# Reading the moving operand of seven products with a step of eight elements, in an attention and mixture-of-experts kernel

## The chip, the cores and the metric

The kernel runs on one core of one Trainium2 chip. The metric is the time of one execution on the device in microseconds. Each kernel is run several times and the median is given. Beside these runs there is one profiled execution, whose trace records every instruction of every engine; its own time is given with it.

The engines of the core work side by side, each through its own queue of instructions: TensorE (PE in the profile; PEld is its loading of the stationary operand), VectorE (DVE), ScalarE (ACT), GpSimd (POOL) and SyncE (SP, which here only issues DMAs). TensorE reads its operands from SBUF and writes PSUM; the stationary operand is loaded first, and the moving operand is then streamed past it, one column after the other.

## The reference

Attention in chunks of 64 tokens gives x of 4608 x 512. Each token then goes to the one of eight experts that its cosine router picks, and is scaled by its gate.

```python
def _attn_ref(q, k, v):                      # (8, 8, 576, 64) each
    q_c = q.reshape(B, H, nc, chunk, D)      # chunk = 64, and k_c, v_c alike
    scores = scale * np.matmul(q_c, k_c.transpose(0, 1, 2, 4, 3))
    attn = np.exp(scores - np.max(scores, axis=-1, keepdims=True))
    attn = attn / (np.sum(attn, axis=-1, keepdims=True) + 1e-09)
    return np.matmul(attn, v_c).reshape(B, H, S, D)

def _moe_ref(x, expert_emb, tau, w1, w2):    # N, D, E, F = 4608, 512, 8, 1024
    logits = xn @ en.T / tau                 # rows of x and expert_emb at norm 1
    expert_idx = np.argmax(logits, axis=1)
    probs = softmax(logits)
    gate_w = probs[np.arange(N), expert_idx]
    for e in range(E):
        mask = expert_idx == e
        h = np.maximum(x[mask] @ w1[e], 0.0)
        out[mask] = gate_w[mask, None] * (h @ w2[e])
```

All operands are float32. The change lies in `x[mask] @ w1[e]` and the maximum with 0 behind it.

## The kernel before

**Two stages.** The first, some 200 us, is attention for 36 tiles of 128 tokens, with the router: each token's row, with its logits and its number, is scattered to a list in device memory (`spots`) that is sorted by expert. The second takes the lists back in blocks of 128 rows: two groups of 64 tokens, `s` = 0 and 1, each of one expert, so that a block can have two experts at once. There are 36 paired blocks and a tail whose number is only known when the kernel runs. The order of the instructions is written out by hand (a manual schedule), so each engine's queue is the order of the calls.

**The first layer of a block** is `hidden_fast` (line 328) for 33 of the blocks. It computes two-by-two blocks with seven products in place of eight: the rows' halves and the weights' halves are first combined (`add_x`, line 307, on the tokens; `add_up`, line 283, on the weights), seven products p1 to p7 are formed, and their sums are the four quarters of the hidden layer. The other blocks use `hidden_part` (line 237), the plain product, which the change leaves as it is.

**A product** (line 335) takes one PSUM bank `ps` of 128 partitions x 256 columns, in rotation out of six. It consists of 8 calls of matmul (line 342): two steps `c` over the contraction, two groups `s`, and two halves `r` of the weights' columns. A call has 128 rows of contraction, 32 columns of the stationary operand (32 tokens of `a`) and 256 columns of the moving operand (256 hidden units of `w`). Its output lies on 32 partitions of the bank, and calls that write different quarters of the partitions run side by side. In the trace each float32 call is two matmuls.

**The order of the columns.** The 256 hidden units of one call are counted `(i k)`: `i` of 32, `k` of 8, with `k` the faster. The second layer needs the hidden layer transposed, 32 x 32 at a time, with the 32 columns of one square being those of one `k`. So the columns have to be brought into the order `(k i)` on the way. Before, the products are computed in the order `(i k)`, and `relu` (line 359) turns it: it reads its input with a step of eight elements and writes it without one.

**Behind the products.** p1 is copied from PSUM to SBUF by ACT (line 377). VectorE adds the others to it (`add`, line 374, each 128 x 256), so that `C` in SBUF holds four quarters. ACT applies the relu to each quarter in two halves of 64 partitions (line 361), eight instructions a block, reading `C` and writing `h`. VectorE transposes `h` to `hT` in two instructions (`turn`, line 368), which read `h` without a step.

**The second layer** is `result` (line 405): 32 calls of 512 columns on line 413, 64 matmuls in the trace, then a scaling by the gate on ACT (line 421), and a scatter of the rows to the output (line 428, on POOL's queue). The loop at line 1121 issues, for each block j, first the products of block j + 1 and then the result of block j, so that TensorE has the result to work on while ACT and VectorE turn the products of the next block.

**Other work in the queues.** In ACT's queue between the relus stand the gate's square root and exponential, each with a load of its table (lines 224 and 231), and, if an expert changes, three copies of its new weights (`take_next`, line 295; copies on line 301 under a condition on a register, line 299). On VectorE the next block's tokens are transposed (line 203, with a step of four elements in its input).

Of the kernel before, what the change touches and what calls it, by code (L numbers as in the profile page):

```python
# [12 lines left out]
AF = mybir.ActivationFunctionType  # L13
# [12 lines left out]
def kernel(  # L26
# [21 lines left out]
    G = P // 2  # L48
    Q = 32
# [226 lines left out]
    def block(s, m, w1=None):  # L276

        if m in TS:
            return sums_sb[s][:, TS.index(m)]
        u, v = UV[m]  # L280
        return (w1 or w1_sb)[s].rearrange("p (u c) (v x) -> p u v c x", u=2, v=2)[:, u, v]
# [22 lines left out]
    def quarters(xT):  # L304
        return xT.rearrange("p (u c) (s b i) -> p u b c s i", u=2, s=2, b=2)
# [17 lines left out]
    def bank(ps_h, shape):  # L323
        tag = f"h{bank_no[0] % 6}"
        bank_no[0] += 1
        return ps_h.tile(shape, FP32, tag=tag, name=tag)

    def hidden_fast(j, ps_h, gate, turn_next, swap_next):

        d = mo[j]  # L330
        x = quarters(d["xT"])
        s1, s2, s3, s4 = d["S"]
        W2 = KF * Q

        def product(a, m):
            ps = bank(ps_h, [P, W2])
            for c in range(KD // 2):
                for s in range(2):
                    w = block(s, m)[:, c].rearrange("p (r x) -> p r x", r=2)
                    for r in range(2):  # L340
                        t0 = G * s + Q * r
                        nc.tensor.matmul(  # L342
                            ps[t0 : t0 + Q],
                            lhsT=a[:, c, s],
                            rhs=w[:, r],
                            start=c == 0,
                            stop=c == KD // 2 - 1,
                        )
            return ps


        last = "_last" if j == LEAST - 1 else ""
        hT = bp.tile([P, KF, P], FP32, tag="hT" + last, name="hT", bufs=1 if last else 2)
        d["hT"] = hT
        C = late_p.tile([P, 4, W2], FP32, tag="C", name="C")
        U, c11, c12, c22 = (C[:, i] for i in range(4))
        h = [late_p.tile([P, 2, W2], FP32, tag=f"h{b}", name=f"h{b}") for b in range(2)]

        def relu(b, v, x):
            for s in range(2):  # L360
                nc.scalar.activation(  # L361
                    h[b][G * v : G * v + G, s].rearrange("p (k i) -> p k i", i=Q),
                    x[G * s : G * s + G].rearrange("p (i k) -> p k i", i=Q),
                    AF.Relu,
                )

        def turn(b):
            nc.vector.transpose(  # L368
                hT.rearrange("p k (s b i) -> p b s k i", b=2, i=Q)[:, b],
                h[b].rearrange("p s (k i) -> p s k i", i=Q),  # L370
            )

        def add(out, a, b, op=ALU.add):
            nc.vector.tensor_tensor(out, a, b, op)  # L374

        p1 = product(x[:, 0, 0], "B11")
        nc.scalar.copy(U, p1)  # L377
        next(gate, None)
        next(gate, None)
        p2 = product(x[:, 1, 0], "B21")  # L380
        add(c11, U, p2)
        next(gate, None)
        relu(0, 0, c11)
        turn_next()
        p3 = product(s4, "B22")
        p5 = product(s1, "T1")
        p6 = product(s2, "T2")
        add(U, U, p6)
        add(c12, U, p5)
        add(c12, c12, p3)  # L390
        relu(0, 1, c12)
        for _ in gate:
            pass
        p7 = product(s3, "T3")
        add(U, U, p7)
        add(c22, U, p5)
        relu(1, 1, c22)
        p4 = product(x[:, 1, 1], "T4")
        swap_next()
        add(U, U, p4, ALU.subtract)  # L400
        relu(1, 0, U)
        turn(0)
        turn(1)
# [42 lines left out]
    with (  # L446
# [577 lines left out]
        for t in range(-3, NT + 3):  # L1024
# [22 lines left out]
            if 0 <= t < NT:  # L1047
                values(t)
                b = (2 * t + 2) // NCB + 1
# [52 lines left out]
    with (  # L1102
# [18 lines left out]
        for j in range(LEAST - 1):  # L1121
            n = j + 2

            def turn_next():
                if n < LEAST:
                    turn_xb(n)
                    if n + XBUF < NJ:
                        load_x(n + XBUF)
                    add_x(n)

            def swap_next():
                if NE <= n < LEAST:
                    take_next(n)
# [93 lines left out]
```

## Time and profile before

| | |
|---|---|
| runs before the change | median 677.75 us of 14 (674.63 to 680.26) |
| profiled execution, whole time | 674.17 us |
| its span, first to last instruction | 672.4 us |
| mean granted TensorE clock | 0.981 |
| line 342, matmuls of the products | 3696, mean 379 ns |
| line 413, matmuls of the result, 512 columns | 2304, mean 594 ns |
| line 361, relu on ACT, 64 x 256 | 264, mean 678 ns, 179.0 us busy |

Matmuls overlap each other, so the busy time of one group of them says little; the time from the start of one stretch to the start of the next does more. The busy share of an engine is taken over the whole span; in the second stage it is read from a window. An instruction's idle time is that of its engine just before it, with the instruction whose end released it.

### The profile page before, as it was taken

What the parts mean: (1) busy time and instruction counts of PE and PEld (TensorE: products, weight loads), DVE (VectorE), ACT (ScalarE), POOL (GpSimd) and SP (SyncE); (2) the same over time, 40 slices, a digit from 0 to 9 for tenths busy, and PEclk for the clock granted to TensorE, in tenths of its full rate; (3) what the DMA queues carried; (4) which work ended last, traced back from release to release, by engine and by line L of the source; (5) the groups of instructions that cost most, each with busy time, mean ns of one, the idle gap of its engine ahead of it and who ended that gap; (6) DMA issues with size and microseconds to landing.
All of it is one profiled execution on the core that took longest, in us unless ns stands there. A gap on an engine that the chain in (4) does not pass through costs nothing. (4 is left out here: it accounts for less than half of the span.)

```text
span 672.4 us, 24844 instructions
## 1 busy us (share of the span) xinstructions
PE 625.5 (93%) x9744; PEld 350.0 (52%) x9744; DVE 421.4 (63%) x1140; ACT 444.5 (66%) x776; POOL 155.4 (23%) x237
## 2 busy tenths in 40 slices
PE   6869999998898979999999999999999999999993
PEld 5658878785443446666434444334444444444441
DVE  4648888986498536557675566767654666564430
ACT  5536767765225847777877867778777777877740
POOL 7828787843310100000100100000001000100101
PEclk9879999998999989999999999999999999999997
DMA  9977999988918711112786111776821114411101
GB/s 253 252 197 218 284 283 292 280 237 339 355 53 295 295 34 46 47 36 92 292 308 224 50 39 45 282 280 216 328 81 56 37 48 164 169 43 34 50 30 36
DMA packets 94590, 112.66 MB, mean 168 GB/s; under 512 B 52364, under 2 KB 72588, under 8 KB 94456
## 3 DMA queue, kind: packets, MB, share of 16 engines
q1 hardware_dynamic: 82728, 72.84, 34.1%
q0 software_dynamic: 11696, 38.04, 16.9%
q8 instruction: 81, 1.33, 0.8%
q14 instruction: 53, 0.43, 0.2%
q10 hardware_dynamic: 32, 0.02, 0.0%
HBM read 334.71 MB, written 22.69 MB: 532 GB/s over the span
## 5 line engine op out<-in xcount | busy, mean ns | idle before, releaser
L413 PE MATMUL y_ps<-w,hT 128*32 128x512 f32 (+1 forms) x2368 | 273.1, 589 | 3.7 <-DMA w<-in_moe_w_dram 3.7
L361 ACT ACTIVATE h<-C 64x256 f32<-64x256 f32 x264 | 179.0, 678 | 95.2 <-DVE C L374 68.7
L413 PEld LDWEIGHTS y_ps<-w,hT 128*32 128x32 f32 x2368 | 93.5, 110 | 153.9 <-issue 123.8
L428 POOL DMA_INDIRECT out_dram<-y,spot x36 | 34.9, 968 | 437.6 <-ACT C L377 186.8
L374 DVE TENSOR_TENSOR C<-C,h 128x256 f32<-128x256 f32 x231 | 96.1, 416 | 49.4 <-DVEq L299 42.6
L342 PE MATMUL h<-w,S 128*32 128x256 f32 x1056 | 98.1, 379 | 1.8 <-DVE w L291 1.8
L342 PE MATMUL h<-sums,xbT 128*32 128x256 f32 x1056 | 97.0, 379 | 0.0
L342 PE MATMUL h<-w,xbT 128*32 128x256 f32 x1056 | 79.4, 380 | 7.1 <-ACTq L299 5.9
L368 DVE STREAM_TRANSPOSE hT<-h 128x512 f32<-128x512 f32 x66 | 46.7, 708 | 44.2 <-ACT h L361 44.1
L342 PEld LDWEIGHTS h<-w,xbT 128*32 128x32 f32 x1056 | 40.9, 110 | 43.2 <-ACTq L299 13.4
L342 PEld LDWEIGHTS h<-w,S 128*32 128x32 f32 x1056 | 49.3, 110 | 24.3 <-DVE w L291 1.5
L342 PEld LDWEIGHTS h<-sums,xbT 128*32 128x32 f32 x1056 | 49.0, 110 | 21.8 <-ACT C L377 0.4
L227 DVE TENSOR_SCALAR rn<-rn 128x1 f32<-128x1 f32 x37 | 5.7, 153 | 72.5 <-ACT rn L224 72.5
L342 PE MATMUL h<-sums,S 128*32 128x256 f32 x528 | 48.7, 379 | 0.0
L682 ACT COPY xT<-tr 128x512 f32<-128x512 f32 x36 | 21.1, 587 | 35.9 <-PE tr L680 35.9
L800 POOL DMA_INDIRECT spots<-xr,dest x36 | 37.1, 1029 | 33.1 <-DVE dest L765 9.9
L203 DVE STREAM_TRANSPOSE xbT<-xin 128x256 f32<-128x256 f32 x73 | 44.3, 645 | 0.5 <-DVE hT L368 0.5
L224 ACT ACT_TABLE_LOAD x34 | 43.6, 1283 | 0.9 <-issue 0.3
L421 ACT ACTIVATE y<-y_ps,gate 128x512 f32<-128x512 f32 (+1 forms) x37 | 25.2, 682 | 28.6 <-issue 15.2
L231 ACT ACT_TABLE_LOAD x34 | 43.6, 1283 | 0.6
L572 POOL DMA_DIRECT2D kx<-in_k_dram x36 | 31.5, 876 | 17.0 <-PE tr L595 16.9
L572 POOL DMA_DIRECT2D qx<-in_q_dram x40 | 34.4, 863 | 0.9 <-PE tr L595 0.6
(202 smaller groups left out, 800.6 us busy)
## 6 DMA issues: line engine op xcount, KB each, us to landing
w<-in_moe_w_dram SPq DMA_DIRECT2D x74, 2048.0 KB
next_w<-in_moe_w_dram SPq DMA_DIRECT2D x67, 2048.0 KB
xin<-spots SPq DMA_DIRECT2D x158, 64.0 KB
qx<-in_q_dram POOLq DMA_DIRECT2D x32, 256.0 KB
v<-in_v_dram SPq DMA_DIRECT2D x56, 144.0 KB
kx<-in_k_dram POOLq DMA_DIRECT2D x28, 256.0 KB
spot<-spots SPq DMA_DIRECT2D x80, 4.0 KB
spots<-blank SPq DMA_DIRECT2D x2, 576.0 KB
```

The costliest lines, as they stand in the source:

```text
L203: nc.vector.transpose(xT[:, :, cols].rearrange("p c (b i) -> p b c i", i=Q), t[:, s * (D // 2) : (s + 1) * (D // 2)].rearrange("p (b i c) ...
L224: nc.scalar.activation(rn, spot[:, j % SPOTS, SQ : SQ + 1], AF.Sqrt)
L231: nc.scalar.activation(sh, sh, AF.Exp, accum_out=gate)
L342: nc.tensor.matmul(ps[t0 : t0 + Q], lhsT=a[:, c, s], rhs=w[:, r], start=c == 0, stop=c == KD // 2 - 1,)
L361: nc.scalar.activation(h[b][G * v : G * v + G, s].rearrange("p (k i) -> p k i", i=Q), x[G * s : G * s + G].rearrange("p (i k) -> p k i", i=Q),
L368: nc.vector.transpose(hT.rearrange("p k (s b i) -> p b s k i", b=2, i=Q)[:, b], h[b].rearrange("p s (k i) -> p s k i", i=Q),)
L374: nc.vector.tensor_tensor(out, a, b, op)
L413: nc.tensor.matmul(ps[Q * r : Q * r + Q, 0:w], lhsT=d["hT"][:, c, Q * t0 : Q * t0 + Q], rhs=w2_sb[s][buf_of(j)][:, c, d0 : d0 + w], start= ...
L421: nc.scalar.activation(y[:, 0:w], ps[:, 0:w], AF.Copy, scale=gate_of.pop(j))
L428: ins = nc.gpsimd.indirect_dma_start(out=to, out_offset=bass.IndirectOffsetOnAxis(ap=at, axis=0), in_=y[:, 0:w], in_offset=None, bounds_ch ...
L572: eng.dma_start(out=x[done : done + n], in_=src[b, :, s : s + n, :].rearrange("h p d -> p h d"),)
L800: ins = nc.gpsimd.indirect_dma_start(out=spots, out_offset=bass.IndirectOffsetOnAxis(ap=at, axis=0), in_=m, in_offset=None, bounds_check=S ...
```

## The change

The step moves from the relu to the products. The moving operand is read in the order `(k i)`, eight runs of 32 elements with a step of eight, so that the columns come to lie in PSUM in the order in which the transposes need them; the relu then reads and writes without a step.

```diff
             for c in range(KD // 2):
                 for s in range(2):
-                    w = block(s, m)[:, c].rearrange("p (r x) -> p r x", r=2)
+
+                    w = block(s, m)[:, c].rearrange("p (r i k) -> p r k i", r=2, i=Q)
                     for r in range(2):
                         t0 = G * s + Q * r
                         nc.tensor.matmul(
-                            ps[t0 : t0 + Q],
+                            ps[t0 : t0 + Q].rearrange("p (k i) -> p k i", i=Q),
                             lhsT=a[:, c, s],
                             rhs=w[:, r],
                             start=c == 0,
...
         def relu(b, v, x):
             for s in range(2):
                 nc.scalar.activation(
-                    h[b][G * v : G * v + G, s].rearrange("p (k i) -> p k i", i=Q),
-                    x[G * s : G * s + G].rearrange("p (i k) -> p k i", i=Q),
-                    AF.Relu,
+                    h[b][G * v : G * v + G, s], x[G * s : G * s + G], AF.Relu
                 )
```

`block(s, m)` is the weights' quarter or combination `m` of group `s`, and `Q` is 32.

## The prediction

> **What bounds the kernel now.** I read the page's busy table and slices first, to find the engine that sets the time, then the window from 504 to 530 us, which holds two whole blocks, then the merged timeline of TensorE in it, then the groups by shape for prices.
>
> ```profile
> span 672.4 us, 24844 instructions
> PE 625.5 (93%) x9744; PEld 350.0 (52%) x9744; DVE 421.4 (63%) x1140; ACT 444.5 (66%) x776; POOL 155.4 (23%) x237
> ...
> PE   6869999998898979999999999999999999999993
> ```
>
> From the sixteenth slice on TensorE is never idle by more than a tenth until the last. ACT, whose work the change lightens, is busy two thirds of the span. The two blocks, split at the border between the products (line 342) and the result (line 413):
>
> ```profile
> core 0: us, PE busy (x) PEld busy (x) DVE busy (x) ACT busy (x) POOL busy (x), PEclk, DMA share, GB/s
> 504.39:510.44 6.05, 6.05 (x117) 3.63 (x113) 3.19 (x10) 5.54 (x10) 0.97 (x1) 1.00 0.19 63
> 510.44:517.30 6.86, 6.86 (x72) 2.15 (x67) 4.00 (x12) 4.07 (x7) 0.00 (x0) 1.00 0.16 40
> 517.30:523.34 6.04, 6.04 (x116) 3.62 (x112) 3.18 (x10) 5.38 (x10) 0.97 (x1) 1.00 0.13 47
> 523.34:530.20 6.86, 6.86 (x70) 2.15 (x66) 3.99 (x12) 3.85 (x7) 0.00 (x0) 1.00 0.17 44
> ```
>
> The columns are the window, its length, each engine's busy time, the granted clock (1.00). TensorE is busy for all of both blocks, and a block lasts 6.04 + 6.86 = 12.90 us; ACT has 9.2 to 9.6 us of work in it, VectorE 7.2. So in a block neither ACT nor VectorE sets the pace. The question is whether TensorE streams at its own rate, or issues:
>
> ```profile
> 517.30 2.10 PE L342 MATMUL h<-w,xbT 128*32 128x256 f32 x30
> 519.03 0.39 PE L342 MATMUL h<-w,S 128*32 128x256 f32 x2
> ...
> 523.34 0.60 PE L413 MATMUL y_ps<-w,hT 128*32 128x512 f32 x2
> ```
>
> Columns: start, length, group. From 517.30 to 523.34 there are seven products of 8 calls. Each call is two matmuls in the trace (1056 + 1056 + 1056 + 528 = 3696 on line 342 for 33 x 56 = 1848 calls), so 112. A call writes a quarter of the partitions, and four run side by side: 112 / 4 = 28 groups of four in 6.04 us, 215.7 ns a group, or 0.843 ns per column of 256. In the result it is 64 matmuls of 512 columns in 6.86 us, 16 groups of 429 ns, 0.837 ns a column. Twice the columns, twice the time: TensorE is bound by the columns streamed, with nothing to spare. Any added nanosecond per column of the products is on the path: there are 33 x 28 = 924 groups, so one nanosecond per group is 0.92 us.
>
> **What the change removes: the step-8 read of the relu.** Prices:
>
> ```profile
> L361 ACT ACTIVATE h<-C 64x256 f32<-64x256 f32 x264 | 179.0, 678 | 95.2 <-DVE C L374 68.7 <-ACTq L299 18.7 <-DVE hT L368 5.5
> L631 ACT ACTIVATE a<-a 128x512 f32<-128x512 f32 x36 | 22.5, 626 | 5.1 <-DVE a L621 5.1
> L301 ACT COPY w<-next_w 128x1024 f32<-128x1024 f32 x18 | 17.7, 1044 | 1.5 <-ACTq L299 1.4
> L377 ACT COPY C<-h 128x256 f32<-128x256 f32 x33 | 12.2, 369 | 2.8 <-PE h L342 2.7
> L263 ACT ACTIVATE h<-h_ps 128x256 f32<-128x256 f32 x8 | 2.6, 381 | 11.8 <-PE h_ps L253 11.8
> ```
>
> Without a step ACT takes 626 ns for 512 elements and 1044 for 1024 from SBUF: 0.816 ns each and 208 ns fixed. So the new relu is 208 + 256 x 0.816 = 417 ns where the old one is 678: 261 ns x 264 = 69 us off ACT. Nearly all lies beside TensorE's stream, as the windows show. What reaches the path is where TensorE waits for ACT: the copies of line 301 when an expert changes stand behind four relus in ACT's queue. In the waits from 250 us on TensorE loses 5.9 us to ACT's queue at line 299 and 0.9 us to line 301. Four relus save 1.04 us, and the longest such wait is 1.3 us, so at best all 6.8 us go; at worst (the copies wait for their DMA instead) nothing. I take 6.8 where the products get longer, since they cover the rest. In the tail nothing is gained: the last relu ends about 644.9 and the last pair's result starts at 650.76, after line 253.
>
> **What it adds: the same step on TensorE's moving operand.** Instruction counts and order on all engines stay, DMAs too; 3696 matmuls now read 8 runs of 32 elements that lie 32 bytes apart, out of the same 256. The output view of `ps` covers the same contiguous columns, at no cost; the seven products are permuted alike, so the additions of line 374 are untouched, and `turn` reads as before. The trace of before has no matmul with a stepped moving operand, so the price is bounded. From below: 215.7 ns a group, no cost. From the other side, rows of other engines that read SBUF with a step:
>
> ```profile
> L368 DVE STREAM_TRANSPOSE hT<-h 128x512 f32<-128x512 f32 x66 | 46.7, 708 | 44.2 <-ACT h L361 44.1
> L203 DVE STREAM_TRANSPOSE xbT<-xin 128x256 f32<-128x256 f32 x73 | 44.3, 645 | 0.5 <-DVE hT L368 0.5
> ...
> L771 DVE TENSOR_REDUCE before<-eqb_all 128x8 bf16<-128x264 bf16 x1 | 0.6, 621 | 0.0
> ...
> L771 DVE TENSOR_REDUCE before<-eqb_all 128x8 bf16<-128x40 bf16 x1 | 0.2, 227 | 0.0
> ```
>
> ACT: (678 - 208) / 256 = 1.84 ns an element; take off the 12 ns that the same pattern costs when it is read from PSUM (381 against 369) and 1.79 remain. VectorE's reduction at a step of 16 bytes: (621 - 227) / 224 = 1.76 ns. VectorE's transpose with a step of four elements takes 645 ns for half the elements that take 708 without one; with 168 ns fixed (from 292 ns for 128 and 416 for 256 elements on lines 318 and 374) that is 1.86 against 1.05. So two engines of different pace both end near 1.8 ns per element. TensorE's columns come at 0.843 ns, almost ACT's 0.816, from the same SBUF with the same step and the same 8 x 32 pattern. I therefore price a stepped column by the ACT row, 1.79 ns: 256 x 1.79 = 458 ns a group, 242 more. The rows around it give, by VectorE's smallest ratio (1.76 / 1.05 = 1.67) 1.67 x 215.7 = 360 ns, and by ACT's largest (1.84 / 0.816 = 2.25) 485.
>
> Here two rules of the Trainium skill bear on the rows. The page "Advanced Engine Details and Errata" (Memory Cachelines) says that SBUF is read in lines of 16 bytes and an access that goes to a new line each time pays; it gives no price, so by it the sum is only some loss, and the stepped ACT and VectorE rows agree that there is one. "TensorE: Matmul & The Clock Gate" (Step-by-step) says that throughput is N cycles for N columns fed, and names no step; by that alone there is no cost and the sum would be 671 us.
>
> **The sum.** Stepped stream: 924 x 242 ns = +224 us. Waits of TensorE behind relus: -6.8 us. The profiled execution took 674.2 us (672.4 of span and 1.8 around it), and the median of the runs, 677.75, lies 3.6 above. 674.2 + 224 - 6.8 = 891 for a profiled execution, **895 us** as a median. The block grows from 12.9 to 19.7 us, in which ACT's work falls to some 7.5 us and VectorE's stays at 7.2, so nothing else takes over.
>
> **The rivals.**
> - *The step costs TensorE nothing* (faster). Four streams read side by side at full rate, so the reading side has some slack per stream that nothing here measures, and TensorE may fetch ahead of its columns. Against it: ACT streams as fast from the same memory and doubles. Then 677.75 - 6.8 = 671 us (678 if the copies wait for their DMA). It decides as long as a group grows by less than 6.8 us / 924 = 7 ns. Chance 0.11.
> - *It is hidden in part*: 1.2 to 1.6 times the group time, 43 to 129 ns more, 40 to 120 us, giving 715 to 794. Nothing in the rows shows so small a penalty at a step of 16 bytes or more. Chance 0.08.
> - *The four streams get in each other's way*: if neighbouring columns come together in one fetch and stepped ones each need their own, the four streams may be served in turn, and a group takes 4 x 215.7 = 863 ns: +598 us, 1,269. For it: four streams of stepped reads are something that no row shows. Against: they do not disturb each other, ACT or VectorE now. Chance 0.11.
> - *The relu does not get faster*, because its 678 ns come from its 64 partitions and not from the step: it changes the 6.8 us alone and moves the forecast to 902, inside its range.
>
> **How the numbers follow.** The likeliest case, TensorE pays per stepped element about what ACT and VectorE pay, has 0.70; by its rows it goes from 360 ns (+133, 805 us) to 485 ns (+249, 920), with a margin 800 to 930. For 8 in 10, the upper half of the partly hidden case is added below and a little above: 750 to 940, which leaves out the case at no cost, most of the case of streams in turn and the lower end of the hidden one. What a measurement of this kernel can tell from no change is about 0.3%, 2 us. Slower: 0.70 + 0.08 + 0.11 less a sliver = 0.88; faster 0.10; the same 0.02, from the free case with its waits kept.
>
> **What would show it.** In the changed kernel's profile line 361's successor should stand near 417 ns; the window of one block's products should be near 12.8 us instead of 6.04, with line 413 unchanged at 6.86 and TensorE still busy throughout; the matmul's own mean should rise from 379 ns by roughly the 242. The granted clock should stay at 1.00 in the blocks; if it falls, part of a loss is the clock's and not the step's. I am wrong in the main step if the products still take 6.04 us; wrong in size if a group is under 360 or over 485 ns; wrong in the small term if TensorE still waits for ACT at line 299 as before.

## The result, and the profile after

The changed kernel takes a median of 885.16 us (882.4 to 886.4, 10 runs), the kernel before 676.18 us over the 47 runs beside it: a ratio of 1.3082, interval 1.3052 to 1.3111. It is slower by almost a third. Its profiled execution took 882.3 us, 880.5 of it span.

The page of the changed kernel, busy table and TensorE's slices:

```profile
span 880.5 us, 24844 instructions
PE 843.6 (96%) x9744; PEld 453.9 (52%) x9744; DVE 428.6 (49%) x1140; ACT 376.3 (43%) x776; POOL 155.3 (18%) x237
...
PE   6699989899999999999999999999999999999994
```

The number of instructions is the same to the last one. ACT has 68 us less to do (376.3 against 444.5), VectorE about as much as before, and TensorE 218 us more. The relu's row, and one row of the products, first after, then before:

```profile
L362 ACT ACTIVATE h<-C 64x256 f32<-64x256 f32 x264 | 109.3, 414 | 210.7 <-DVE C L373 208.0
...
L343 PE MATMUL h<-sums,xbT 128*32 128x256 f32 x1056 | 139.9, 642 | 0.0
```

```profile
L342 PE MATMUL h<-sums,xbT 128*32 128x256 f32 x1056 | 97.0, 379 | 0.0
```

The relu fell from 678 to 414 ns, as its row without a step said. What it won turned into idle time: ACT now waits 208 us for VectorE's additions (68.7 before), and these wait 82.2 us for TensorE (3.3 before). The matmul went from 379 to 642 ns, 263 more; matmuls overlap, so it is the group of four below that sets the time. One block, by the windows of the changed kernel, products first and result second, and its products in TensorE's timeline (start, length, group):

```profile
637.49:650.40 12.91, 12.91 (x117) 6.18 (x113) 5.60 (x17) 6.29 (x13) 0.97 (x1) 1.00 0.14 43
650.40:657.28 6.88, 6.88 (x68) 3.14 (x64) 1.79 (x4) 1.05 (x3) 0.00 (x0) 1.00 0.01 4
```

```profile
641.16 2.12 PE L343 MATMUL h<-w,S 128*32 128x256 f32 x16
643.00 2.12 PE L343 MATMUL h<-sums,xbT 128*32 128x256 f32 x16
644.85 2.12 PE L343 MATMUL h<-sums,S 128*32 128x256 f32 x16
```

The products of a block take 12.91 us instead of 6.04; the result takes 6.88, against 6.86 before. The granted clock (1.00, the number behind POOL's busy time) has not moved. The result takes as long as before, so the loss is not the clock's. From one product's start to the next it is 1.845 us, in which four groups of four matmuls run: 461 ns a group against 215.7, or 1.80 ns a column against 0.843.

The whole difference can be made up from the starts of the 33 blocks' products. In the changed kernel the 32 intervals between them are all 19.78 to 19.82 us. Before, most are 12.91, but 13 of 32 are longer, and the 32 add up to 19.0 us over 32 x 12.91. This surplus is called the excess from here on. So the span should grow by 33 x (19.795 - 12.910) = 227.2 us and shrink by the 19.0 of the excess: 208.2. It grew by 880.5 - 672.4 = 208.1.

### The profile page after: what moved, and what is told of

Read it like the earlier page. It is cut to its first block, busy times and chain, and to the rows that moved or that the text cites. A ratio compares the mean times of both kernels' runs of the same rounds, so it can differ in the third digit from the quotient of the medians.

```text
span 880.5 us, 24844 instructions
## 1 busy us (share of the span) xinstructions
PE 843.6 (96%) x9744; PEld 453.9 (52%) x9744; DVE 428.6 (49%) x1140; ACT 376.3 (43%) x776; POOL 155.3 (18%) x237
## 2 busy tenths in 40 slices
DMA packets 94590, 112.66 MB, mean 128 GB/s; under 512 B 52364, under 2 KB 72588, under 8 KB 94456
## 4 chain that ended last, share of the span: by engine, by line
issue 72%; POOL 4%; DVE 0%; POOLq 0%; ACT 0%; ACTq 0%
POOL out_dram L427 4%; POOLq L427 0%; DVE sums L291 0%; DVE S L318 0%; DVE hT L268 0%; POOLq L137 0%; ACT C L376 0%; DVE xbT L318 0%; ACT y L420 0%; ACT h L263 0%; ACTq L376 0%; POOLq L1180 0%; POOLq L1185 0%; ACTq L224 0%; ACTq L263 0%
## 5 line engine op out<-in xcount | busy, mean ns | idle before, releaser
L412 PE MATMUL y_ps<-w,hT 128*32 128x512 f32 (+1 forms) x2368 | 260.4, 587 | 0.0
L362 ACT ACTIVATE h<-C 64x256 f32<-64x256 f32 x264 | 109.3, 414 | 210.7 <-DVE C L373 208.0
L412 PEld LDWEIGHTS y_ps<-w,hT 128*32 128x32 f32 x2368 | 119.3, 112 | 132.7 <-issue 124.7
L373 DVE TENSOR_TENSOR C<-C,h 128x256 f32<-128x256 f32 x231 | 97.1, 420 | 128.0 <-PE h L343 82.2
L343 PE MATMUL h<-sums,xbT 128*32 128x256 f32 x1056 | 139.9, 642 | 0.0
L343 PE MATMUL h<-w,S 128*32 128x256 f32 x1056 | 139.7, 641 | 0.0
L343 PE MATMUL h<-w,xbT 128*32 128x256 f32 x1056 | 130.2, 639 | 0.0
L343 PEld LDWEIGHTS h<-w,xbT 128*32 128x32 f32 x1056 | 56.0, 124 | 63.6 <-issue 55.8
L343 PE MATMUL h<-sums,S 128*32 128x256 f32 x528 | 69.9, 642 | 0.0
L343 PEld LDWEIGHTS h<-sums,S 128*32 128x32 f32 x528 | 29.0, 129 | 32.0 <-issue 32.0
L650 PE MATMUL pv<-v,aT 64*64 64x65 f32 x1152 | 28.5, 229 | 9.3 <-DMA v<-in_v_dram 7.8
```

What stands on the lines that cost most here:

```text
L343: nc.tensor.matmul(ps[t0 : t0 + Q].rearrange("p (k i) -> p k i", i=Q), lhsT=a[:, c, s], rhs=w[:, r], start=c == 0, stop=c == KD // 2 - 1,)
L362: nc.scalar.activation(h[b][G * v : G * v + G, s], x[G * s : G * s + G], AF.Relu)
L412: nc.tensor.matmul(ps[Q * r : Q * r + Q, 0:w], lhsT=d["hT"][:, c, Q * t0 : Q * t0 + Q], rhs=w2_sb[s][buf_of(j)][:, c, d0 : d0 + w], start= ...
L650: nc.tensor.matmul(pv[CH * c : CH * c + CH, par, i], lhsT=d["aT"][r0 : r0 + CH, i, CH * c : CH * c + CH], rhs=v_t[b][r0 : r0 + CH, i, cb, ...
```

## The experiments

They ask four things: which half of the change does what, what of the step it is that costs, whether the four streams share the cost, and whether the relu's gain is to be had without it. They ran on three chips, each with runs of the kernel before beside it (medians of 688.17, 688.47 and 676.54 us). Chips differ in the first stage: the first block starts between 201 and 207 us on the last of the three, and between 218 and 229 us on the other two. So totals are compared on one chip only, and between chips the intervals of the blocks. The totals in the expectations were reckoned from 676 us, and on the first two chips they come out some 12 us low for that reason. A group's time is (interval of blocks - 6.87 us of result) / 28.

**The relu alone**, against the kernel before:

```diff
-                    h[b][G * v : G * v + G, s].rearrange("p (k i) -> p k i", i=Q),
-                    x[G * s : G * s + G].rearrange("p (i k) -> p k i", i=Q),
-                    AF.Relu,
+                    h[b][G * v : G * v + G, s], x[G * s : G * s + G], AF.Relu
```

> The relu's half of the change alone: products as before, relu without a step, so that the hidden units meet the wrong rows of the second layer's weights. In the trace of before, 32 intervals from block to block on TensorE add up to 19 us more than 32 x 12.91; in the changed kernel this excess is gone. Theory: the excess was waiting for ACT, which the shorter relu alone ends: about 676 - 19 = 657 us, blocks all near 12.91. Rival 1: only the 6.8 us of waits that the prediction counted go: 669. Rival 2: the waits were covered by the longer products, not by the faster relu, so without them they stay: 676.

Measured: 680.96 us beside 688.17 for before, ratio 0.9887 (0.983 to 0.9943). The blocks' excess is 3.65 us. A gain of 7 us: rival 1's 6.8, not the 19 of the theory. On this chip the first block starts at 225.2 us, against 202.3 in the trace of before, and no trace of before was taken on it, so the two kernels together were run again later (below).

**The products alone**: the change to lines 339 and 343 without that of the relu.

> The products' half alone: moving operand with a step of 8, relu still reading with a step as before (the order of the hidden units is then wrong). Theory: the longer products cover ACT's waits by themselves: 885 us, equal to the changed kernel, a block of products near 12.93 us. Rival: the faster relu is what removed the waits, so they come back here: up to 19 us more, 904.

Measured: 905.6 us beside 688.17, ratio 1.3174 (1.31 to 1.3249). The total equals the rival's number, but that is the chip's doing: the first block starts at 224.6 us here and at 202.0 in the changed kernel's trace. The 32 intervals add up to 633.7 us here and to 633.5 there, so the faster relu gives the changed kernel nothing in this stage. The longer products alone cover ACT: from the first block on, no wait of TensorE shows in this trace.

**The step moved to the output in PSUM**, the moving operand read without a step, the relu as in the change. The lines are those of the changed kernel and of this one:

```diff
-                    w = block(s, m)[:, c].rearrange("p (r i k) -> p r k i", r=2, i=Q)
+                    w = block(s, m)[:, c].rearrange("p (r i k) -> p r i k", r=2, i=Q)
...
-                            ps[t0 : t0 + Q].rearrange("p (k i) -> p k i", i=Q),
+                            ps[t0 : t0 + Q].rearrange("p (k i) -> p i k", i=Q),
```

> The same column order by another way: moving operand without a step, the output written to PSUM with a step of 32 columns, relu without a step. Theory: the cost of the change lies in reading SBUF with a step, so a stepped write costs nothing: a group of four matmuls stays at 216 ns, 657 us. Rival: the step costs on whichever side it stands: a group at about 460 ns, 880 us. The Trainium skill (Advanced Engine Details and Errata, Memory Cachelines) says that any non-contiguous pattern in PSUM slows matmuls significantly, without a price.

Measured: 681.02 us beside 688.17, ratio 0.9881 (0.9812 to 0.9951). One row of its products, and its timeline of TensorE:

```profile
L342 PE MATMUL h<-sums,xbT 128*32 128x256 f32 x1056 | 94.4, 379 | 0.3 <-ACT C L375 0.3
```

```profile
503.43 0.39 PE L342 MATMUL h<-sums,xbT 128*32 128x256 f32 x2
...
504.30 0.39 PE L342 MATMUL h<-sums,S 128*32 128x256 f32 x2
```

0.87 us from product to product, 217 ns a group (216 by the median interval of 12.91), and the matmul still has 379 ns. The theory's group is met and its total is not: as with the relu alone, 7 us are gained and not 19. Neighbouring columns now land 128 bytes apart in PSUM, and it costs nothing that shows. So what costs is the read of SBUF and not the step as such. The Trainium skill ("Advanced Engine Details and Errata", Memory Cachelines) says that any non-contiguous pattern in PSUM slows matmuls significantly; for this float32 matmul, the measurement says otherwise, and it decides.

**The step made smaller.** The changed kernel with `i=64` (a step of 4 elements) and with `i=128` (a step of 2) in both patterns.

> The changed kernel with a step of 4 elements (16 bytes) in place of 8, in 4 runs of 64 (the order of the hidden units is then wrong). Theory: every element that has no neighbour within 16 bytes pays a fixed time near 1.80 ns, so the step makes no difference: a group at 462 ns, 885 us. Rival: the cost grows with the bytes spanned: half the span, about 231 ns a group, 671 us.

> The changed kernel with a step of 2 elements (8 bytes), in 2 runs of 128 (the order of the hidden units is then wrong). Theory: a fetch of 16 bytes now serves two columns, 1.80 / 2 = 0.90 ns a column against 0.843 at full pace: a group at 216 to 231 ns, 657 to 671 us. Rival: any step at all costs the full price: 462 ns, 885 us.

Measured: 897.22 us beside 688.17 with a step of 4, and 698.04 beside 688.47 with 2, one run each. First the timeline with a step of 4, then the one with 2:

```profile
501.97 0.74 PE L342 MATMUL h<-sums,xbT 128*32 128x256 f32 x2
...
503.78 0.74 PE L342 MATMUL h<-sums,S 128*32 128x256 f32 x2
```

```profile
500.65 0.39 PE L342 MATMUL h<-sums,xbT 128*32 128x256 f32 x1
...
501.56 0.39 PE L342 MATMUL h<-sums,S 128*32 128x256 f32 x1
```

With a step of 4 it is 1.81 us from product to product; over the blocks (median interval 19.65 us) a group takes 456 ns. Half the distance between columns and the price is whole, so the cost does not grow with the distance. With a step of 2 it is 0.91 us; by the median interval of 13.28 us a group takes 229 ns, or 0.894 ns a column, half of 1.79.

**Pairs**: two neighbouring columns, then on by eight, so that a call reads 128 separate pieces of two columns. The new lines, in place of those of the changed kernel:

```diff
+                    w = block(s, m)[:, c].rearrange("p (r i k e) -> p r k i e", r=2, i=Q, e=2)
...
+                            ps[t0 : t0 + Q].rearrange("p (k i e) -> p k i e", i=Q, e=2),
```

> The changed kernel reading two neighbouring columns and then going on by 8, in 4 x 32 pairs (the order of the hidden units is then wrong). Theory: two columns for each fetch, as with a step of 2: 216 to 231 ns a group, 657 to 671 us. Rival: what costs is a jump of 32 bytes or the number of separate runs: half the elements jump, about 340 ns a group, 770 us, or more with 128 runs to begin.

Measured: 698.95 us beside 688.47.

```profile
500.79 0.42 PE L342 MATMUL h<-sums,xbT 128*32 128x256 f32 x2
...
501.71 0.42 PE L342 MATMUL h<-sums,S 128*32 128x256 f32 x2
```

0.92 us from product to product, and 231 ns a group by the median interval of 13.33. Jumps of 32 bytes between pairs cost what a step of 2 costs. So the price hangs on how many columns come from the same small piece of memory: one alone costs 1.78 to 1.80 ns, two together 0.89 to 0.90 each, and neighbours in long runs (of 32, below, or of 256, as before) the 0.84 that TensorE had before. Two columns 8 bytes apart still share a piece, and two 16 bytes apart do not. The Trainium skill (same page and section) states this rule as lines of 16 bytes in SBUF, of which two hits are needed to absorb the latency. The runs agree in the main, and add the price on TensorE: 1.8 ns a line, so that two float32 hits still fall short of the full pace by 6 to 7%.

**Two of the four streams with the step** (`r` = 0), the other two without, against the changed kernel:

```diff
+                    w1 = block(s, m)[:, c].rearrange("p (r k i) -> p r k i", r=2, i=Q)
...
-                            rhs=w[:, r],
+                            rhs=(w, w1)[r][:, r],
```

> Two of the four streams that run side by side with a step of 8, the other two without (the order of half the hidden units is then wrong). Theory: each stream pays for its own elements, and the four start together, so a group takes as long as its slowest: 462 ns, 885 us. Rival: the four share what the step exhausts: the mean of 216 and 462, 339 ns a group, 771 us.

Measured: 907.87 us beside 688.47.

```profile
L343 PE MATMUL h<-sums,xbT 128*32 128x256 f32 x1056 | 178.0, 519 | 0.0
```

```profile
507.52 0.63 PE L343 MATMUL h<-sums,xbT 128*32 128x256 f32 x4
...
509.39 0.63 PE L343 MATMUL h<-sums,S 128*32 128x256 f32 x4
```

1.87 us from product to product, 467 ns a group: no better than with four, where the mean of the two would be 339. The matmul's mean of 519 ns is that of two kinds: in the trace half of them take 379 to 404 ns, about as without a step, and half some 630 to 660, side by side. So the streams do not share what the step exhausts; each pays its own price, and the group ends with its slowest. That a lone stream would pay the same was not tried.

**No step anywhere**, by loading the second layer's weights in another row order, so that a call reads eight runs of 32 neighbouring columns (core of the diff, against the kernel before):

```diff
-    w2_rows = moe_w2.rearrange("e (p c) d -> p e (c d)", c=KF)
+    w2_rows = moe_w2.rearrange("e (v c x) d -> e v x c d", v=2, c=KF)
...
+            for v in range(2):
+                nc.sync.dma_start(
+                    out=w2_sb[s][buf_of(j)][G * v : G * v + G],
+                    in_=w2_rows[ds(e, 1), v].rearrange("o x c d -> (o x) c d"),
+                    cond=f > 0,
+                )
...
-                    w = block(s, m)[:, c].rearrange("p (r x) -> p r x", r=2)
+                    w = block(s, m)[:, c].rearrange("p (k r i) -> p r k i", r=2, i=Q)
```

> No step anywhere: the rows of the second layer's weights are loaded in another order (two DMAs of 64 partitions in place of one of 128), so that runs of 32 neighbouring columns of the first layer's weights, 64 columns apart, are what a call reads; relu without a step, also in the plain product. The output is the reference's. Theory: runs of 32 cost nothing, 216 ns a group, and the excess between blocks is gone: 657 us, and under before. Rival 1: each run's beginning costs a fetch, 8 x 1 to 2 ns a group, 7 to 15 us: 664 to 672. Rival 2: the pieces of 2 KB and the twofold DMA issues on SyncE's queue come late: as before or slower, over 676.

Measured: 746.39 us beside 688.47, ratio 1.0827 (1.0799 to 1.0855). Runs of 32 cost nothing: the undisturbed blocks take 12.91 us, and the matmul 379 ns. The time is lost elsewhere, where rival 2 looked. The largest of TensorE's waits in this kernel's second stage (releaser; us in total, times, longest):

```profile
PE y_ps L420 <- DMA w<-in_moe_w_dram: 37.4, 7, 8.3
```

The same 112.7 MB now come in 103,040 packets in place of 94,590, and the hardware queue's packets take 40.0% of 745 us of the DMA engines' time where they took 34.1% of 672. The blocks' excess is 63 us, which holds these waits, and the mean granted clock is down at 0.946. That the second layer's weights come late is shown; whether the smaller pieces or the twofold issues make them late is not.

**The kernel before, the relu alone, the stepped write and the change, on one chip.**

> The kernel before, unchanged, on the chip of the runs beside it, so that its trace can be held against theirs. In the first trace of before the intervals between blocks had 19 us over 32 x 12.91, part of it a wait of 3.7 us for the second layer's weights by DMA and not for ACT. Theory: the ACT part, some 7 us, is there on every chip and the DMA part is not: an excess of 10 to 12 us here, against 3.6 in the run with the relu alone. Rival: the excess is all the relu's, 19 us here too.

> The relu's half alone once more, on the same chip as the kernel before beside it (the order of the hidden units is wrong). Theory: an excess of about 3.6 us between blocks, as in its first run, some 7 us under the kernel before. Rival: its first run's 3.6 us came from that chip, and it has as much excess as before here.

> The stepped write to PSUM again, with more rounds. Theory: the products cost no more than before and the relu is faster, so it gains what the relu alone gains: a ratio of 0.988 to the kernel before. Rival: its first ratio was luck, and it is the same as before within 0.3%.

> The changed kernel on the same chip. Theory: its second stage does not depend on the chip, 32 blocks of 19.79 us, and what differs between chips lies before the first block. Rival: the blocks themselves change with the chip.

Measured, beside a median of 676.54 us for before: one run of before 671.52, of the relu alone 671.69, of the change 883.79; the stepped write 669.34 over 6 runs, ratio 0.9889 (0.9868 to 0.991). The excess of the 32 intervals over 12.91 us each, split behind the fourth, from where on TensorE's waits before are those behind ACT alone (below):

| | first 4 | other 28 | all |
|---|---|---|---|
| before | 6.8 | 11.2 | 18.0 |
| relu alone | 8.4 | 3.8 | 12.2 |
| stepped write | 7.8 | 3.7 | 11.5 |

The expectation for before (10 to 12 us in all) was wrong: 6.8 us in the first four intervals are there on this chip too, while the relu's first run, on the other chip, had none of it. It is not the same wait each time, though: for weights by DMA TensorE waits 0.2 us there in before and 3.6 in the stepped write, on the same chip. What sets this part stays open. The expectation for the relu alone (3.6 us in all) was wrong for the same reason. The other 28 intervals answer to the relu: 7.4 us less here, and the 3.65 us of the first run are all in them. The two single runs of before and of the relu alone are equal in time, though the stage is 5.8 us shorter, because the first block started 5.7 us later in the one than in the other; runs of before scatter by as much. TensorE's waits from 260 us on, first before, then the stepped write, both on this chip:

```profile
PE h L342 <- ACTq L299: 6.0, 7, 1.3
PE h L342 <- ACT w L301: 0.9, 1, 0.9
```

```profile
PE h L342 <- ACTq L299: 0.6, 3, 0.3
PE h L342 <- ACT C L375: 0.3, 1, 0.3
PE h L342 <- ACT w L301: 0.2, 1, 0.2
```

6.9 us became 1.1. The 6.9 are the copies of an expert's new weights that stood behind the relus; of the 1.1, 0.3 is p1's copy (line 375 here). The changed kernel's blocks on this chip add up to 633.5 us, as in its first trace, and those of the products alone on another chip to 633.7: that stage is not what differs between chips. Writing PSUM with the step is faster than both kernels, than the one before by 1.1%, and that is the relu's gain: its intervals are those of the relu alone within 0.7 us.

## Why the prediction was right

- *TensorE sets the pace of a block by its columns, with nothing to spare*: right. The block grew by 6.885 us, all but 0.02 of it in the products, and the span by 33 times that less the excess.
- *A stepped column costs what ACT pays, 1.79 ns*: right, in size too. A group took 461 ns where 458 was put; the 33 blocks gained 227.2 us where 224 was put. That the price goes over in nanoseconds, and not as a ratio (which gave the lower bound of 360), was argued there from the like pace and pattern of ACT; the run shows it. The runs with steps of 4 and 2 and with pairs suggest why rows of two other engines could price it: on TensorE the price belongs to the fetch from SBUF, 1.8 ns when one element is used of it, and not to the distance. This fits VectorE's reduction, whose 1.76 with 16 bytes is near ACT's with 32. On ACT and VectorE no step was varied, so that all three engines pay for the same thing is likely and not shown.
- *The relu falls to 417 ns and this lies beside TensorE's stream*: right, 414, and without it (the products alone) the blocks take as long.
- *Waits of TensorE behind relus: -6.8 us*: right for the relu, mis-sized as a term. The relu removes 7.4 us of excess in the later 28 intervals. But the changed kernel loses all of the 19.0, since its products give every latecomer 6.9 us more time. Besides ACT these were VectorE's combinations at line 291 (1.8 us) and, in the third interval, a wait of 3.7 us for weights by DMA. I had read the waits from 250 us on, while the blocks start at 202, and had counted ACT's alone. The window around that DMA wait, of before, shows what stood outside my view:

```profile
236.00:250.00 14.00, 10.31 (x93) 5.00 (x89) 5.16 (x16) 4.75 (x8) 0.00 (x0) 0.88 0.12 31
```

TensorE is idle for 3.7 of the 14 us, and the granted clock is 0.88 where the windows on either side have 1.00. The result behind the wait is slow as well: 8.5 us from its start to the next products, in place of 6.9. Sum of the terms: 3 us too little for the stream and 12 too much left for the waits, 9 net, which with the unlike distance of median and profile (3.6 put, 2.8 found) is the 10 us between 895 and 885. That the two misses go opposite ways, and 3 us come off the 12, is luck.

- *The rivals*: no cost falls with the 461 ns. Hidden in part falls as well, for a step of 8; a step of 2 is such a case, smaller still than its bounds (229 ns, 1.06 times). Streams in turn would have needed 863 ns, and the run with two stepped streams shows that they do not share the price. The doubt about the 64 partitions falls with the 414 ns. Two bounds do not follow from the terms beside them: with -6.8 us for the waits, 40 to 120 us give 711 to 791 and not 715 to 794, and 133 us give 804 and not 805. The forecast does not rest on them.

## What to carry to other kernels

Price a stepped read by the nearest row of any engine that reads the same memory with a step, in nanoseconds per element (here 458 ns a group against 461 measured), and hold it against the pace at which the new reader takes its elements: the cost is the difference, and it counts where that reader sets the time. Where a step has to stand somewhere, put it on the side or the engine where it is free, here the write to PSUM, and not where it is merely out of sight. When a stage gets longer, count all the waits in it as cover that may go, from its first instruction on, whoever is late.

## What the runs showed of the hardware

- A float32 matmul that writes PSUM with a step of 32 columns takes 379 ns, as without a step.
- One float32 column used of a fetch costs 1.78 to 1.80 ns on TensorE (steps of 4 and 8); two, 0.89 to 0.90 each, whether they are 8 bytes apart or neighbours; runs of 32 keep the full pace of 0.843.
- Four stepped streams side by side take 461 ns a group, and two stepped beside two plain ones 467, with the plain matmuls at 379 to 404 ns and the stepped ones at some 630 to 660: each stream pays for itself, and nothing is gained by mixing.
